# Permuting the q and k columns and adding product blocks before the logits matmuls in the two middle chunks

## The chip, the core and the metric

The kernel runs on one core of a Trainium2 chip. The core has five engines with instruction streams of their own: TensorE (PE in the profile; its weight loads are listed as PEld), VectorE (DVE), ScalarE (ACT), GpSimd (POOL) and SyncE (SP). They meet only at semaphores. Matmul results go to PSUM, all other data lie in SBUF. The metric is the device time of one launch in microseconds. The times before were 264.53, 264.16 and 264.13 us, median 264.16.

## The reference

Input x has 2048 rows (tokens) of 640 elements, type bf16. Two branches work on the layer norm of x, and both are added to x.

```
xn  = layernorm(x)
qkv = xn @ wqkv                       # 32 heads of 20 elements
for token s, head h, w in 0..7:       # window of 8, dilation 2
    logits[s,h,w] = sum_d q[s,h,d] * k[s-2w,h,d] * 20**-0.5   (masked where s-2w < 0)
attn = softmax over w
o[s,h,:] = sum_w attn[s,h,w] * v[s-2w,h,:]
out = x + o @ wo + ((xn @ w_gate) * (xn @ w_up)) @ w_down     # 1536 hidden columns
```

## The kernel before

The 2048 tokens are cut into four chunks of 512, and each chunk into four token tiles of 128. A row of 640 is five blocks of 128 partitions (KT = 5).

For a chunk, TensorE does these things:
- `qk` (L405): q and k, transposed, so that a partition is a column of q or k and the 512 tokens lie along the free dimension. For each of the five blocks, five matmuls of 512 columns. Their weights are 128 neighbouring columns of wq or wk. ScalarE copies the results out of PSUM (L412).
- `vproj` (L438): v, one token tile at a time. It is stored to a scratch tensor vD in HBM, from where VectorE's operand for the values is loaded with the eight window positions side by side (L556, issued on SP).
- the logits (L492, below),
- `glu` (L623): gate and up, 12 pairs of groups of five matmuls. ScalarE copies them out (L628), VectorE multiplies them to hT (L639).
- `down` (L664 and L667): for each token tile, two halves of 320 columns. Each half is 12 matmuls with hT and wd and five with the attention output oT and wo, into one PSUM bank. VectorE adds x on the way out (L674). For the first tile of a chunk the last two hT matmuls of each half come after both halves' other matmuls.

The logits are made in two steps (`prodlog`). VectorE multiplies q by k shifted by 0, 2, ... 14 tokens: eight products of 128 partitions x 2560 elements (five blocks of 512 tokens), two to a tile `pw` (L476). TensorE then sums them over the 20 elements of each head with a selector matrix Ek of zeros and ones: for each block i the selector `Ek[:, i, :]` says which head each of the 128 columns of that block belongs to. A matmul has 32 columns of weights (heads) and 512 of tokens, four of them work side by side in four column strips of the array, and five blocks accumulate. So one group of four products is 20 matmuls, and a chunk has two groups.

ScalarE copies the logits out (L505), the SP queue transposes them (LT, L513), VectorE takes the maximum and subtracts it (L524 to L528), ScalarE takes the exponential, VectorE sums and normalizes (L541 to L546). `av` then multiplies the loaded values by the weights (L581), adds the eight positions in a tree (L590, L594, L596) and a transpose on SP makes oT (L603).

The order of the work is made by a planner. Each step is given with an engine, an estimated cost, its dependencies and sometimes an order. `Plan.order` lists the steps, at each time taking the ready one with the least slack to the end. The logits steps are marked `urgent`: they go first on TensorE as soon as the plan counts them ready, with 0.9 us added after the last product (`margin`). The engines then run their streams in exactly that order. In the order before, the logits of chunk 0 lie before its last v tiles, those of chunk 1 among the q matmuls of chunk 2, those of chunk 2 before the last tile of the chunk-1 down-projection, those of chunk 3 after the first part of the chunk-2 down-projection.

Five buffers (`pv`) hold the four `pw` tiles and one loaded value tile. Value tiles two to four of a chunk go into buffers that the logits matmuls release. Matmul results rotate through six PSUM banks, which ScalarE and VectorE empty.

Of the kernel before, what the change touches and what calls it, by code (L numbers as in the profile page):

```python
# [10 lines left out]
ALU = mybir.AluOpType  # L11
# [20 lines left out]
class Plan:  # L32
# [8 lines left out]
    def add(self, eng, cost, fn, deps=(), occ=None, after=(), kb=0):  # L41
        s = Step(eng, cost, fn, deps, occ, after)
        s.kb = kb
        s.idx = len(self.steps)
        self.steps.append(s)
        return s
# [51 lines left out]
def kernel(  # L98
# [11 lines left out]
    nc = tc.nc  # L110
    P = nc.NUM_PARTITIONS
# [4 lines left out]
    H = 32  # L116
    Dh = D // H
# [5 lines left out]
    KT = D // P  # L123
# [4 lines left out]
    CS = CH * P  # L128
    JL = P // H
    NS = D // 2  # L130
    BF, F32 = dt.bfloat16, dt.float32
    assert D == KT * P and F == FT * P and S == NCH * CS and W * H == 2 * P and Dh == JL * KT

    const = ctx.enter_context(tc.tile_pool(name="const", bufs=1))
# [5 lines left out]
    wq = const.tile([P, KT, D], BF, name="wq")  # L140
    wk = const.tile([P, KT, D], BF, name="wk")
# [4 lines left out]
    wd = const.tile([P, FT, D], BF, name="wd")  # L146
    ident = const.tile([P, P], BF, name="ident")
    mhalf = const.tile([P, 1], F32, name="mhalf")
    Ek = const.tile([P, KT, H], BF, name="Ek")
    negm = const.tile([P, 2, HALO], F32, name="negm")  # L150
    vD = dram.tile([HALO + S, D], BF, name="vD")

# [1 line left out]
    add = plan.add  # L154
    T = {}

    def new(key, shape, dtype, tag, bufs, pool=None):
        t = (pool or sb).tile(shape, dtype, name=tag, tag=tag, bufs=bufs)
        T[key] = t
        return t  # L160
# [10 lines left out]
    def wload(dst, src, eng=None):  # L171
        return lambda: (eng or nc.sync).dma_start(out=dst[:], in_=src.rearrange("(i p) f -> p i f", p=P))
# [31 lines left out]

    def consts_e():
        nc.gpsimd.memset(Ek[:], 1.0)
        nc.gpsimd.affine_select(out=Ek[:], in_=Ek[:], pattern=[[P, KT], [-Dh, H]], compare_op=ALU.is_ge,
                                fill=0.0, base=0, channel_multiplier=1)
        nc.gpsimd.affine_select(out=Ek[:], in_=Ek[:], pattern=[[-P, KT], [Dh, H]], compare_op=ALU.is_ge,
                                fill=0.0, base=Dh - 1, channel_multiplier=-1)  # L210

    def consts_m():
        nc.gpsimd.memset(negm[:], 0.0)
# [95 lines left out]
    def pe_main(cost, fn, deps=(), banks=1):  # L309
        nonlocal main  # L310
        waits = []
        for k in range(banks):
            if len(ring) + k >= 6:
                waits.append(ring[len(ring) + k - 6])
        main = add("PE", cost + 0.165, fn, [main, *waits, *deps], occ=cost)
        return main
# [79 lines left out]
    def qk(c, lo, n, rs=(0, 1)):  # L396
        for r in rs:
            for j in range(KT):
                key = ("qk", c, r, j, lo)

                def pe(i0, i1, key=key, r=r, j=j):
                    if i0 == 0:
                        new(key, [P, 512], F32, "ps", 6, psum)
                    for i in range(i0, i1):
                        nc.tensor.matmul(T[key][:, 0:n], lhsT=(wk if r else wq)[:, i, j * P : (j + 1) * P],  # L405
                                         rhs=T["xnT", c][:, i, lo : lo + n], start=(i == 0), stop=(i == KT - 1))

                def ev(key=key, r=r, j=j):
                    if r == 0 and j == 0 and lo == 0:
                        new(("q", c), [P, KT, CS], BF, "q", 2)  # L410
                    dst = T["k", c][:, j, HALO + lo : HALO + lo + n] if r else T["q", c][:, j, lo : lo + n]
                    nc.scalar.copy(dst, T[key][:, 0:n])  # L412

                one = n / 2400 + 0.0027
                ts = range(c * CH + lo // P, c * CH + (lo + n) // P)
                mine = [WK if r else WQ, *[TX.get(t, TT[t]) for t in ts], LASTPW.get(c - 2)]
                if c or r or j:
                    a = pe_main(KT * one, lambda pe=pe: pe(0, KT), mine + [TT[t] for t in ts])
                else:
                    pe_main(3 * one, lambda pe=pe: pe(0, 3), mine)  # L420
                    a = pe_main(2 * one, lambda pe=pe: pe(3, KT), [TT[t] for t in ts], banks=0)
                e = add("ACT", 0.16 + n / 1200, ev, [a, HALOCP[c]], occ=0.07 + n / 1200)
                ring.append(e)
                (Kk if r else Q).setdefault(c, []).append(e)
# [38 lines left out]


    SPLAST = [None]
    PW, LL, LE, SS, DD, AA, O16, OE, V8, DT = {}, {}, {}, {}, {}, {}, {}, {}, {}, {}

    def prodlog(c):
        for g in range(2):
            for j in range(4):  # L470
                i = 4 * g + j

                def mul(i=i):
                    if i % 2 == 0:
                        new(("pw", c, i // 2), [P, 2, KT, CS], BF, "pv", 5)
                    nc.vector.tensor_tensor(T["pw", c, i // 2][:, i % 2, :, :], T["q", c][:],  # L476
                                            T["k", c][:, :, DIL * i : DIL * i + CS], ALU.mult)

                m = 8 * c + i
                w = [LL.get(2 * c - 1), O16.get(4 * c - 4), O16.get(4 * c - 3), O16.get(4 * c - 2)][i // 2]  # L480
                PW[m] = add("DVE", 1.48, mul, [*Q[c], *Kk[c], w], occ=1.395, after=[PW.get(m - 1) if i else V8.get(4 * c - 1)])
        LASTPW[c] = PW[m]
        if c == 0:
            load_v8(0)
        for g in range(2):
            n = 2 * c + g

            def lg(g=g):
                l = new(("lps", c, g), [P, 512], F32, "pl", 2, psum)
                for i in range(KT):  # L490
                    for j in range(4):
                        nc.tensor.matmul(l[H * j : H * (j + 1), :], lhsT=Ek[:, i, :], rhs=T["pw", c, 2 * g + j // 2][:, j % 2, i, :],  # L492
                                         start=(i == 0), stop=(i == KT - 1), tile_position=(0, H * j),
                                         skip_group_check=True)

            LL[n] = add("PE", 1.25, lg, [PW[m], LL.get(n - 1), LE.get(n - 2), LE.get(n - 1 - g), CE], occ=1.12)
            LL[n].urgent = True
            LL[n].margin = 0.9

            def ev(g=g):  # L500
                L = new(("L", c, g), [P, CS], BF, "L", 2)
                if c == 0:
                    ps = T["lps", c, g]
                    nc.vector.tensor_tensor(ps[:, 0:HALO], ps[:, 0:HALO], negm[:, g, :], ALU.add)
                nc.scalar.copy(L[:], T["lps", c, g][:])  # L505

            LE[n] = add("ACT", 0.585, ev, [LL[n], SS.get(n - 2), CM], occ=0.5)

            def tr(g=g):
                if g == 0:  # L510
                    new(("LT", c), [P, CH, W, H], BF, "LT", 1)
                out = T["LT", c][:].rearrange("p t (g w) h -> p t g (w h)", g=2)[:, :, g, :]
                nc.sync.dma_start_transpose(out=out, in_=T["L", c, g][:])  # L513

            early = [SPLAST[0]] if c == 0 else []
            SS[n] = SPLAST[0] = add("SP", 3.5, tr, [LE[n], DD.get(2 * c - 1), DD.get(2 * c - 2)], occ=1.25, after=early, kb=160)

# [32 lines left out]
    def load_v8(t):  # L550
        def fn():
            v = new(("v8", t), [P, W, D], BF, "pv", 5)
            r0 = t * P
            src = vD[r0 : r0 + P, :]
            src = bass.AP(tensor=src.tensor, offset=src.offset, ap=[[D, P], [DIL * D, W], [1, D]])
            nc.sync.dma_start(out=v[:], in_=src)  # L556
        order = [SPLAST[0]] if t < CH - 1 else [SS[2 * (t // CH) + 1]] if t % CH in (1, 2) else []
        c, u = divmod(t, CH)
        order.append(V8[t - 1] if u else PW[8 * c + 6])
        if t == 3:  # L560
            order.append(WL["o"])
        w = LL[2 * c + (u - 1) // 2] if u else O16.get(t - 1)
        V8[t] = add("SP", 6.0, fn, [VS[t], VS.get(t - 1), w, CZ], occ=0.5, after=order, kb=1280)
        if t < 3:
            SPLAST[0] = V8[t]
            V8[t].floor = (40.0, 0, 0)[t]

    def load_down():
        WL["d"] = SPLAST[0] = add("SP", 8, wload(wd, B_w_down), after=[SPLAST[0]], occ=0.5, kb=1920)

    def load_out():
        WL["o"] = SPLAST[0] = add("SP", 8, wo_load, after=[SPLAST[0]], occ=2.7, kb=1100)

# [134 lines left out]
    a = st_in(0, 0)  # L708
    a = st_in(0, 1, a)
    aggr_in(0, a)  # L710
    a = st_in(1, 0)
    a = st_in(1, 1, a)
# [10 lines left out]
    a = st_in(2, 0)  # L723
    a = st_in(2, 1, a)
# [6 lines left out]
    a = st_in(3, 0)  # L731
    a = st_in(3, 1, a)
# [9 lines left out]
    CE = add("POOL", 1.2, consts_e, [C0, RS[3]])  # L742
# [77 lines left out]
```

## Time and profile before

| | before |
|---|---|
| median of three runs | 264.16 us |
| span of the profiled execution | 263.0 us |
| TensorE busy, of the span | 258.2 us, 98% |
| VectorE busy | 214.6 us, 82% |
| ScalarE busy | 106.1 us, 40% |
| one chunk's logits on TensorE | 2.27 us for 40 matmuls |
| one product on VectorE (L476) | 1484 ns, 32 of them |
| TensorE's granted clock | 1.000 |

The profile gives one execution. Its span runs from the first to the last instruction; it states no device time of its own beside that, and the median of the runs is 1.16 us above the span. "Busy" counts the time in which an engine has an instruction in work; a share of busy time is an average over stages with different limits. The chain that ended last is followed back from the last instruction, at each step to what released it. In groups, the first number behind the bar is the total busy time in us, the second the mean of one in ns, and behind the next bar stands the time that the engine sat idle just before, with the releaser.

### The profile page before, as it was taken

What the parts mean: (1) busy time and instruction counts of PE and PEld (TensorE: products, weight loads), DVE (VectorE), ACT (ScalarE), POOL (GpSimd) and SP (SyncE); (2) the same over time, 40 slices, a digit from 0 to 9 for tenths busy, and PEclk for the clock granted to TensorE, in tenths of its full rate; (3) what the DMA queues carried; (4) which work ended last, traced back from release to release, by engine and by line L of the source; (5) the groups of instructions that cost most, each with busy time, mean ns of one, the idle gap of its engine ahead of it and who ended that gap; (6) DMA issues with size and microseconds to landing.
All of it is one profiled execution on the core that took longest, in us unless ns stands there. A gap on an engine that the chain in (4) does not pass through costs nothing.

```text
span 263.0 us, 4102 instructions
## 1 busy us (share of the span) xinstructions
PE 258.2 (98%) x1574; PEld 140.4 (53%) x1574; DVE 214.6 (82%) x337; ACT 106.1 (40%) x197; POOL 39.4 (15%) x84
## 2 busy tenths in 40 slices
PE   7999999999999999999999999999999999999995
PEld 2645445444577546444477554644456764445763
DVE  5586997999999969999999189999992999993221
ACT  3655557655300258455500155655541105554000
POOL 4551036000031021400001000420000004000000
PEclk9999999999999999999999999999999999999999
DMA  7978997999978139931167299451903995111001
GB/s 217 326 175 231 402 373 171 370 362 244 195 155 270 54 68 370 316 114 27 25 125 250 66 311 319 97 150 25 224 3 75 365 293 134 26 25 25 27 25 50
DMA packets 50707, 46.55 MB, mean 177 GB/s; under 512 B 24786, under 2 KB 47840, under 8 KB 50688
## 3 DMA queue, kind: packets, MB, share of 16 engines
q1 hardware_dynamic: 46704, 37.10, 50.0%
q0 software_dynamic: 2384, 8.05, 9.2%
q10 hardware_dynamic: 1600, 1.15, 1.4%
q8 instruction: 12, 0.20, 0.3%
q14 instruction: 7, 0.06, 0.1%
HBM read 35.39 MB, written 5.26 MB: 155 GB/s over the span
## 4 chain that ended last, share of the span: by engine, by line
PE 94%; DMA 3%; DVE 1%; issue 0%
PE ps L623 39%; PE ps L664 20%; PE ps L405 17%; PE ps L667 8%; PE ps L438 7%; PE pl L492 3%; DMA wq<-in_A_wqkv_dram 3%; DMA x<-in_A_x_dram 1%; DVE st L251 1%; DVE xr L674 0%; DVE mv L257 0%; DVE ve L259 0%; DVE x L270 0%
## 5 line engine op out<-in xcount | busy, mean ns | idle before, releaser
L623 PE MATMUL ps<-xnT,wg 128*128 128x512 bf16 x240 | 59.6, 379 | 0.0
L623 PE MATMUL ps<-xnT,wu 128*128 128x512 bf16 x240 | 59.6, 379 | 0.0
L664 PE MATMUL ps<-wd,hT 128*128 128x320 bf16 (+2 forms) x384 | 57.4, 299 | 0.0
L476 DVE TENSOR_TENSOR pv<-q,k 128x2560 bf16<-128x2560 bf16 x32 | 46.5, 1484 | 1.7 <-ACT k L412 1.7
L664 PEld LDWEIGHTS <-hT 128*128 128x128 bf16 x384 | 37.0, 98 | 16.5 <-issue 0.8
L581 DVE TENSOR_TENSOR pv<-pv,a 128x5120 bf16<-128x5120 bf16 x16 | 45.1, 2819 | 0.1
L628 ACT CAST gs<-ps 128x512 bf16<-128x512 f32 x48 | 28.2, 587 | 32.1 <-PE ps L623 32.1
L623 PEld LDWEIGHTS <-wu 128*128 128x128 bf16 x240 | 23.5, 98 | 28.3
L623 PEld LDWEIGHTS <-wg 128*128 128x128 bf16 x240 | 23.5, 98 | 27.7
L628 ACT CAST us<-ps 128x512 bf16<-128x512 f32 x48 | 28.2, 588 | 22.4 <-PE ps L623 21.4
L674 DVE TENSOR_TENSOR xr<-ps,xr 128x320 bf16<-128x320 f32 (+2 forms) x32 | 15.0, 486 | 24.4 <-PE ps L667 16.1
L667 PE MATMUL ps<-wo,oT 128*128 128x320 bf16 (+2 forms) x160 | 27.0, 299 | 0.0
L698 POOL DMA_DIRECT2D out_dram<-xr x14 | 7.6, 545 | 124.6 <-DVE xr L674 118.0
L590 DVE TENSOR_TENSOR pv<-pv 128x2560 bf16<-128x2560 bf16 x16 | 23.8, 1485 | 0.1
L438 PE MATMUL ps<-wv,xnT 128*128 128x320 bf16 x160 | 23.2, 299 | 0.4 <-ACT xnT L351 0.4
L412 ACT CAST q<-ps 128x512 bf16<-128x512 f32 x20 | 11.7, 586 | 28.3 <-PE ps L405 28.3
L639 DVE TENSOR_TENSOR hT<-gs,us 128x512 bf16<-128x512 bf16 x48 | 19.5, 419 | 4.1 <-ACT us L628 4.1
L405 PE MATMUL ps<-xnT,wq 128*128 128x512 bf16 x100 | 22.4, 379 | 0.4 <-DMA wq<-in_A_wqkv_dram 0.4
L405 PE MATMUL ps<-xnT,wk 128*128 128x512 bf16 x100 | 22.2, 379 | 0.0
L438 PEld LDWEIGHTS <-xnT 128*128 128x128 bf16 x160 | 15.3, 98 | 7.4 <-ACT xnT L351 0.5
L667 PEld LDWEIGHTS <-oT 128*128 128x128 bf16 x160 | 15.5, 98 | 6.3
L251 DVE BATCH_NORM_STATS2 st<-x 128x6 f32<-128x320 bf16 x32 | 13.9, 481 | 4.4 <-DMA x<-in_A_x_dram 4.4
(54 smaller groups left out, 177.4 us busy)
## 6 DMA issues: line engine op xcount, KB each, us to landing
pv<-vD SPq DMA_DIRECT2D x16, 1280.0 KB, 9.9
vD<-v_t POOLq DMA_DIRECT2D x16, 160.0 KB, 4.5
xr<-in_A_x_dram POOLq DMA_DIRECT2D x16, 160.0 KB, 3.6
out_dram<-xr POOLq DMA_DIRECT2D x14, 160.0 KB, 3.7
wg<-in_B_w_gate_dram SPq DMA_DIRECT2D x1, 1920.0 KB, 8.1
wu<-in_B_w_up_dram SPq DMA_DIRECT2D x1, 1920.0 KB, 11.9
wd<-in_B_w_down_dram SPq DMA_DIRECT2D x1, 1920.0 KB, 14.6
x<-in_A_x_dram SPq DMA_DIRECT2D x11, 160.0 KB, 6.8
```

What stands on the lines that cost most here:

```text
L251: nc.vector.bn_stats(T["st", t][:, g, :], T["x", t][:, g * NS : (g + 1) * NS])
L405: nc.tensor.matmul(T[key][:, 0:n], lhsT=(wk if r else wq)[:, i, j * P : (j + 1) * P], rhs=T["xnT", c][:, i, lo : lo + n], start=(i == 0), ...
L438: nc.tensor.matmul(T["psv", t, n][:, 0:NS], lhsT=T["xnT", c][:, i, q * P : (q + 1) * P], rhs=wv[:, i, n * NS : (n + 1) * NS], start=(i == ...
L476: nc.vector.tensor_tensor(T["pw", c, i // 2][:, i % 2, :, :], T["q", c][:], T["k", c][:, :, DIL * i : DIL * i + CS], ALU.mult)
L581: nc.vector.tensor_tensor(v[:].rearrange("p w (j h) -> p w j h", j=Dh, h=H), v[:].rearrange("p w (j h) -> p w j h", j=Dh, h=H), T["a", n][ ...
L590: nc.vector.tensor_tensor(v[:, 0:4, :], v[:, 0:4, :], v[:, 4:8, :], ALU.add)
L623: nc.tensor.matmul(ps[:], lhsT=(wu if r else wg)[:, i, f * P : (f + 1) * P], rhs=T["xnT", c][:, i, :], start=(i == 0), stop=(i == KT - 1))
L628: nc.scalar.copy(s[:], T[key][:])
L639: nc.vector.tensor_tensor(h[:], T["gs", c, f][:], T["us", c, f][:], ALU.mult)
L664: nc.tensor.matmul(ps, lhsT=T["hT", c, f][:, q * P : (q + 1) * P], rhs=wd[:, f, sl], start=(f == 0), stop=(f == FT - 1 and not wo_part))
L667: nc.tensor.matmul(ps, lhsT=T["oT", t][:, g, :], rhs=wo[:, g, sl], start=False, stop=(g == KT - 1 and f1 == FT))
L674: nc.vector.tensor_tensor(T["xr", t][:, sl], T["psD", t, n][:, 0:w], T["xr", t][:, sl], ALU.add)
```

## The change

The weights of q and k are no longer 128 neighbouring columns but every fifth column: block j takes columns j, j + 5, j + 10, and so on. Partition p of block j then holds column 5p + j, which belongs to head p // 4 whatever j is. So one selector of 32 columns serves all five blocks, and blocks may be added to each other, partition by partition, before the selector is applied.

In chunks 1 and 2 (`LEVELS`), after each pair of products, `fold` lets VectorE add blocks 2 and 3 of a `pw` tile to its blocks 0 and 1, in place: one instruction over both products of the tile, 2 x 1024 elements per partition, four instructions in a chunk. The logits of these chunks then sum three blocks (0, 1 and 4) in place of five: 24 matmuls a chunk in place of 40. Chunks 0 and 3 keep five. The path over GpSimd in `fold` and the deeper levels are not used.

The logits step now depends on the folds, and the planner is given its new cost, so the order changes around it. Chunk 1's logits come after 25 q and 15 k matmuls of chunk 2 (before: after 20 q). Chunk 2's come after the whole chunk-1 down-projection and the 25 q matmuls of chunk 3 (before: ahead of the last down tile). Chunk 3's come ahead of the last half tile of the chunk-2 down-projection (before: after the first of its eight halves, of 10 + 5 matmuls). On VectorE the folds of chunk 1 stand together behind its products, those of chunk 2 stand in pairs between evictions, and the first product of the next chunk moves ahead of the softmax sums in chunks 1 and 2. On SP the four xnT transposes of chunk 3 come ahead of the last oT transpose of chunk 1. GpSimd's order is the same.

```diff
-    Ek = const.tile([P, KT, H], BF, name="Ek")
+    Ek = const.tile([P, H], BF, name="Ek")
...
-        nc.gpsimd.affine_select(out=Ek[:], in_=Ek[:], pattern=[[P, KT], [-Dh, H]], compare_op=ALU.is_ge,
+        nc.gpsimd.affine_select(out=Ek[:], in_=Ek[:], pattern=[[-JL, H]], compare_op=ALU.is_ge,
...
-                        nc.tensor.matmul(T[key][:, 0:n], lhsT=(wk if r else wq)[:, i, j * P : (j + 1) * P],
+                        nc.tensor.matmul(T[key][:, 0:n], lhsT=(wk if r else wq)[:, i, :].rearrange("p (c b) -> p c b", b=KT)[:, :, j],
...
+    LEVELS = (0, 1, 1, 0)
+    FOLDER = ('DVE', 'DVE', 'DVE', 'DVE')
+    LEFT = (tuple(range(KT)), (0, 1, KT - 1), (0, KT - 1), (0,))
+    HALVES = ((0, 2, 2, 4), (0, 1, 1, 2), (0, 1, KT - 1, KT))
+
+    def fold(c, u):
+        s = PW[8 * c + 2 * u + 1]
+        for lo, hi, a, b in HALVES[: LEVELS[c]]:
+            def fn(lo=lo, hi=hi, a=a, b=b):
+                w = T["pw", c, u]
+                if FOLDER[c] == "DVE":
+                    nc.vector.tensor_tensor(w[:, :, lo:hi, :], w[:, :, lo:hi, :], w[:, :, a:b, :], ALU.add)
...
+            n = (hi - lo) * 2 * CS
+            if FOLDER[c] == "DVE":
+                s = add("DVE", 0.25 + n / 1920, fn, [s], occ=0.165 + n / 1920)
...
+                if i % 2:
+                    FO[4 * c + i // 2] = fold(c, i // 2)
...
-                for i in range(KT):
+                left = LEFT[LEVELS[c]]
+                for i in left:
                     for j in range(4):
-                        nc.tensor.matmul(l[H * j : H * (j + 1), :], lhsT=Ek[:, i, :], rhs=T["pw", c, 2 * g + j // 2][:, j % 2, i, :],
-                                         start=(i == 0), stop=(i == KT - 1), tile_position=(0, H * j),
+                        nc.tensor.matmul(l[H * j : H * (j + 1), :], lhsT=Ek[:], rhs=T["pw", c, 2 * g + j // 2][:, j % 2, i, :],
+                                         start=(i == left[0]), stop=(i == left[-1]), tile_position=(0, H * j),
...
-            LL[n] = add("PE", 1.25, lg, [PW[m], LL.get(n - 1), LE.get(n - 2), LE.get(n - 1 - g), CE], occ=1.12)
+            took = 0.022 + 0.2195 * len(LEFT[LEVELS[c]])
+            LL[n] = add("PE", took + 0.13, lg, [*[FO[4 * c + u] for u in range(4)], LL.get(n - 1), LE.get(n - 2), LE.get(n - 1 - g), CE], occ=took)
```

More of the change, by code (lines that the diff above doesn't have):

```diff
@@ L206, in consts_e @@
         nc.gpsimd.memset(Ek[:], 1.0)
-        nc.gpsimd.affine_select(out=Ek[:], in_=Ek[:], pattern=[[P, KT], [-Dh, H]], compare_op=ALU.is_ge,
+        nc.gpsimd.affine_select(out=Ek[:], in_=Ek[:], pattern=[[-JL, H]], compare_op=ALU.is_ge,
                                 fill=0.0, base=0, channel_multiplier=1)
-        nc.gpsimd.affine_select(out=Ek[:], in_=Ek[:], pattern=[[-P, KT], [Dh, H]], compare_op=ALU.is_ge,
-                                fill=0.0, base=Dh - 1, channel_multiplier=-1)
+        nc.gpsimd.affine_select(out=Ek[:], in_=Ek[:], pattern=[[JL, H]], compare_op=ALU.is_ge,
+                                fill=0.0, base=JL - 1, channel_multiplier=-1)
     def consts_m():
@@ L465 @@
     SPLAST = [None]
+    FO = {}
     PW, LL, LE, SS, DD, AA, O16, OE, V8, DT = {}, {}, {}, {}, {}, {}, {}, {}, {}, {}
+    LEVELS = (0, 1, 1, 0)
[9 more added lines that the diff above has]
+                    nc.vector.tensor_tensor(w[:, :, lo:hi, :], w[:, :, lo:hi, :], w[:, :, a:b, :], ALU.add)
+                else:
+                    nc.gpsimd.dma_start(out=w[:, :, lo:hi, :], in_=w[:, :, a:b, :], accum_op=ALU.add)
+            n = (hi - lo) * 2 * CS
+            if FOLDER[c] == "DVE":
+                s = add("DVE", 0.25 + n / 1920, fn, [s], occ=0.165 + n / 1920)
+            else:
+                s = add("POOL", 4.0, fn, [s], occ=1.2, kb=n / 4)
+        return s
     def prodlog(c):
```

## The prediction

> **What bounds the kernel now.** First the head of the page, the busy shares, the slices and the chain that ended last.
>
> ```profile
> span 263.0 us, 4102 instructions
> PE 258.2 (98%) x1574; PEld 140.4 (53%) x1574; DVE 214.6 (82%) x337; ACT 106.1 (40%) x197; POOL 39.4 (15%) x84
> ...
> PE   7999999999999999999999999999999999999995
> ...
> DVE  5586997999999969999999189999992999993221
> PEclk9999999999999999999999999999999999999999
> ...
> PE 94%; DMA 3%; DVE 1%; issue 0%
> ```
>
> TensorE holds 94% of the chain, at full granted clock in every slice. VectorE is at nine tenths for long stretches, with holes near slices 23 and 31. So time taken from TensorE is worth its full length, as long as VectorE, which receives new work, still delivers each operand before TensorE asks for it. That is a question of slack at a few places, so I read the chain in order of time next, then VectorE's timeline at the same places (start, duration, then the work; in brackets the idle time before it).
>
> ```profile
> 69.06 1.36 PE ps L664 x10
> ...
> 78.29 1.63 PE ps L664 x12
> ...
> 87.53 4.32 PE ps L405 x20
> 91.85 2.27 PE pl L492 x40
> 94.12 6.58 PE ps L405 x30
> 100.70 5.43 PE ps L438 x40
> 106.13 25.90 PE ps L623 x120
> ...
> 133.39 0.68 PE ps L667 x5
> ...
> 145.89 2.27 PE pl L492 x40
> 148.16 1.74 PE ps L664 x12
> ...
> 169.11 25.90 PE ps L623 x120
> ...
> 197.05 2.27 PE pl L492 x40
> 199.32 1.47 PE ps L664 x10
> ...
> 258.20 1.08 PE ps L667 x5
> ```
>
> ```profile
> 89.18 1.48 DVE L476 TENSOR_TENSOR pv<-q,k 128x2560 bf16<-128x2560 bf16 x1
> 90.58 2.45 DVE L251 BATCH_NORM_STATS2 st<-x 128x6 f32<-128x320 bf16 x6
> ...
> 94.08 1.49 DVE L270 TENSOR_SCALAR x<-x,mv,rstd 128x640 bf16<-128x640 bf16 x3
> 97.54 0.29 DVE L524 TENSOR_TENSOR m<-LT 128x256 bf16<-128x256 bf16 x1 [1.98 <-DMA LT<-L]
> ...
> 103.16 2.83 DVE L581 TENSOR_TENSOR pv<-pv,a 128x5120 bf16<-128x5120 bf16 x1
> ...
> 130.20 0.49 DVE L596 TENSOR_TENSOR o<-pv 128x640 bf16<-128x640 bf16 x1
> ...
> 140.49 0.48 DVE L674 TENSOR_TENSOR xr<-ps,xr 128x320 bf16<-128x320 f32 x1
> 140.89 1.48 DVE L476 TENSOR_TENSOR pv<-q,k 128x2560 bf16<-128x2560 bf16 x1
> ...
> 151.66 0.29 DVE L524 TENSOR_TENSOR m<-LT 128x256 bf16<-128x256 bf16 x1 [0.56 <-DMA LT<-L]
> ```
>
> **The terms.** The groups by shape (busy total, mean ns) carry the prices:
>
> ```profile
> L590 DVE TENSOR_TENSOR pv<-pv 128x2560 bf16<-128x2560 bf16 x16 | 23.8, 1485 | 0.1
> L594 DVE TENSOR_TENSOR pv<-pv 128x1280 bf16<-128x1280 bf16 x16 | 13.1, 821 | 0.2
> L639 DVE TENSOR_TENSOR hT<-gs,us 128x512 bf16<-128x512 bf16 x48 | 19.5, 419 | 4.1 <-ACT us L628 4.1
> L528 DVE TENSOR_TENSOR d<-LT,m 128x512 f32<-128x512 bf16 x8 | 5.5, 692 | 0.3
> L405 PEld LDWEIGHTS <-wk 128*128 128x128 bf16 x100 | 9.8, 98 | 11.8
> L444 ACT CAST v_t<-ps 128x320 bf16<-128x320 f32 x32 | 13.3, 430 | 7.4 <-PE ps L438 4.1 <-DMA vD<-v_t 3.3
> L412 ACT CAST k<-ps 128x512 bf16<-128x512 f32 x20 | 11.7, 586 | 9.4 <-PE ps L405 9.4
> ```
>
> Last, the DMA issues (median us to landing) and two stretches of SP's timeline:
>
> ```profile
> pv<-vD SPq DMA_DIRECT2D x16, 1280.0 KB, 9.9
> ...
> oT<-o SPq DMA_TRANSPOSE x16, 2.8
> ```
>
> ```profile
> 96.40 3.81 SPq L556 DMA_DIRECT2D pv<-vD  x3
> ...
> 132.06 5.16 SPq L339 DMA_TRANSPOSE xnT<-x  x4
> ```
>
> *Removed from TensorE.* A chunk's logits are 40 matmuls in 2.27 us. Chunks 1 and 2 keep 24, so 24/40 x 2.27 = 1.36 us, 0.91 us less each and 1.82 us together. Chunks 0 and 3 keep 40. The 0.1 us lost on returning from logits to other matmuls (1.74 for 12 matmuls at 148.16, 0.11 over the 1.63 of other such groups) stays.
>
> *Added to VectorE.* Four in-place adds of 2048 elements per partition in each of the two chunks. Between the in-place rows of 2560 and 1280 elements the slope is (1485 - 821)/1280 = 0.519 ns, so one takes 1485 - 512 x 0.519 = 1219 ns. Independent neighbours overlap by 0.08 us (the product of 89.18 lasts 1.48 and its successor starts 1.40 later), so one add occupies 1.14 us: 4.56 us per chunk, 9.1 us in all. Bounds: at the f32 row's 512 elements in 692 ns (below one element per ns) an add would be near 692 + 1536/512 x 692 = 2.77 us; at the in-place rate 1.22. I take 1.22, since type, engine and in-place form are those of the nearer rows.
>
> *Weights with a column step of five.* 200 loads of q, k weights now read every fifth column. No row shows a stepped weight load. Packed ones take 98 ns, beside matmuls that start 4.32/20 = 0.216 us apart, so a load is free up to 216 ns. ScalarE's copy of 320 elements with a large step costs 430 ns against 586 for 512 packed ones; the difference, 156 ns for 192 elements or 0.81 ns each, leaves 430 - 320 x 0.81 = 170 fixed, the same as 586 - 512 x 0.81 = 171: there the step is free. By that 98 ns, by a doubling (two elements read for one) 196; both hide, so zero, with nothing on the gain side as packed loads are hidden already. [...] The sum is the same unless the slowed load passes the 216 ns, which is a rival below. No run so far shows it.
>
> *Constants.* The selector shrinks from 160 to 32 columns on POOL, far from the path: zero. Each selector load still precedes its matmul.
>
> **What the new order moves.** The planner puts logits 1 behind 25 q and 15 k matmuls, logits 2 behind the whole chunk-1 down-projection and 25 q matmuls, logits 3 before the last half tile of the chunk-2 down. One product of the following chunk goes ahead of the softmax sums in chunks 1 and 2. I follow VectorE against TensorE, place by place.
>
> *Logits 1.* TensorE reaches them at 87.53 + 40 x 0.216 = 96.17. The products end as before, four adds follow: 90.58 + 3 x 1.14 + 1.22 = 95.22. Slack 0.95, the smallest.
>
> *Softmax and values of chunk 1.* Logits end 97.53. Before, the maximum started 3.42 after their end (94.12 to 97.54: eviction, transpose), so 100.95; VectorE, with its layer norm 4.56 later, is free at 95.57 + 4.56 = 100.1. From maximum to first value multiply 5.62, plus the inserted product 1.40, less the idle 0.23 it fills: 107.7. From there to the last output 27.53 (103.16 to 130.69), plus two more hT multiplies (0.42 less the overlap each), 0.67: 135.9. TensorE finishes gate and up at 106.13 - 0.91 + 25.90 = 131.12. It needs the tenth hT then; What follows that hT on VectorE is 0.82 + 0.49 + 2.83 + 0.67 + 1.49 + 0.82 + 0.49, with overlaps 7.5, so it is ready at 128.4, slack 2.7. The value loads of token tiles two to four, which need the logits' buffers, are issued 2.3 us after the logits' end as before (96.40), so from 99.8; the second multiply comes at 107.7 + 5.7 = 113.4, 13.6 later, against 9.9 to landing. The last output's transpose, now queued on SP behind four xnT transposes that wait for gate and up to finish (131.1 plus 5.16 us of issue, the row at 132.06), leaves at 136.4 and lands 2.8 later, before about 146.6 when the last token tile asks for it.
>
> *Logits 2.* Down lasted 87.53 - 69.06 = 18.47, so it ends at 149.59; 25 q matmuls more, 154.99. VectorE from 135.9: 7 products x 1.40, 8 evictions x 0.40, 4 adds x 1.14 = 17.6, hence 153.5, or 153.6 with the last add's tail. Slack 1.4. TensorE then runs 1.36 + 0.1 + 5.39 + 5.43 to gate and up at 167.3 (169.11 before), ending 193.2.
>
> *Values of chunk 2.* Maximum at 156.35 + 3.50 = 159.85, values from 166.6, last output 194.8. Behind the tenth hT stand 1.49 + 0.82 + 0.49 and two hT, 3.4 with overlaps: 191.4 against 193.2, slack 1.8.
>
> *Chunk 3.* Its products end near 206.4; logits 3 start at 193.18 + 18.47 - 2.31 (a half tile, 1.63 + 0.68) = 209.34, slack 2.9. Their end 211.61 is 12.3 later than before. Maximum at 215.0, last output at 215.0 + 5.39 + 27.53 + 0.67 = 248.6, its transpose 2.8 later, 251.4. TensorE needs it for the group that stood at 258.20, now 256.4: slack 5. So what falls late everywhere is VectorE, and TensorE meets each operand in time.
>
> **The sum.** The span is 263.0 - 1.82 = 261.2. The profiled execution shows no device time of its own beside the span; the runs shown have a median of 264.16, 1.16 above it, which I keep: 262.34. About 0.2% of the time, 0.53 us, is what can be told from no change.
>
> **The rivals.**
>
> *VectorE comes late (faster by little, or no change).* For: slacks of 0.95 and 1.4 where nine tenths are busy, and logits 3 moved by 12 us. Against: the adds are of a shape well bracketed, and all other waits keep 1.8 or more. Adds priced like the 2560 row (1.49) would take 4 x 1.40 = 5.6 and end at 96.3, a stall of 0.1. A further lateness of 1 us at two places costs up to 1.5: 262.8 to 264.5.
>
> *A weight load longer than its matmul (slower).* The place is the 200 q, k loads, each beside a 216 ns matmul. A load of L costs 200 x (L - 216) ns on TensorE; from 225 ns on it eats the 1.82. At three times the packed time, 294 ns, it costs 15.6 us: 262.34 + 15.6 = 277.9; at 235 ns 266.1. For: nothing in the trace shows a stepped load. Against: more than a doubling is needed. [...]
>
> *Adds at f32 rate (slower or level).* 2.77 us each puts logits 1 at 90.58 + 11.0 = 101.6, a stall of 5.4, and part of it again at logits 2: 264.16 - 1.82 + 5.4 = 267.7 or more. Against: both in-place bf16 rows.
>
> *The change does less than it says.* If four matmuls side by side cost more per group when fewer follow, the gain is under 0.91 a chunk; even at half of it 263.25.
>
> **How the numbers follow.** The forecast, 262.34, has 0.71, its own range 262.0 to 262.8. VectorE late 0.13, spread evenly from 262.8 to 264.5. The smaller gain 0.03. Weight loads 0.08 and slow adds 0.05, above 264.7. The range 261.9 to 264.4 leaves out the two slower cases and a little. Faster takes the forecast, the smaller gain and about half of the late case, 0.80; no change the rest of the late case, 0.07; slower 0.13.
>
> **What would show it.** Adds near 1.22 us, x8. Logits groups of 24 in 1.36 us, starting near 96.2 and 155.0, with TensorE's wait list empty of VectorE there. Weight loads on the q, k line near 98 and below 216 ns, their 50 matmuls still 10.8 us per chunk. Maximum of chunk 3 near 215, last output near 249, the last tile's first wo group near 256.4. A wait of TensorE for VectorE at logits or at the down-projection, or q, k matmuls spaced beyond 0.216, would make the prediction wrong.

## The result and the profile after

The changed kernel takes 262.63 us in the median of four runs (262.45 to 263.31), beside 264.33 for the kernel before (264.13 to 264.53, four runs). The ratio is 0.994, with a 95% interval of 0.9926 to 0.9955: 1.70 us less. The forecast was 262.3.

The head of the page of the changed kernel, with the lines that answer to those shown of before:

```profile
span 261.6 us, 4046 instructions
PE 256.6 (98%) x1542; PEld 143.7 (55%) x1542; DVE 223.0 (85%) x345; ACT 104.8 (40%) x197; POOL 38.8 (15%) x84
...
DVE  5586996999999995999999973989999819999941
PEclk9999999999999999999999999999999999999999
...
PE 90%; DMA 5%; DVE 4%; POOL 0%; issue 0%; SPq 0%
```

TensorE has 32 matmuls less and still holds the chain. VectorE has 8.4 us more busy time. Its two holes have moved with the later logits, from slice 23 to 25, where it is now three tenths busy and not one, and from slice 31 to 33. The part of the chain outside TensorE grew in the first 25 us: chunk 0's logits start at 36.99 here and at 36.70 before. That is not the work of the new order, for two kernels of the experiments with the same order start them at 36.03 and 36.37. From the start of these logits to the end of the span it is 226.3 us before and 224.6 now, 1.7 us less. This profiled execution, 263.31 us, is also the longest of the four. It lies 1.7 us above its span, as the profiled execution of the first experiment does (264.02 over 262.3). With 1.7 the profiled execution of before, span 263.0, would be one of 264.7 us, longer than the four timed. So the 1.16 us that the prediction kept between span and median probably paired a longer execution with the median of others. Only differences went into the sum, so nothing hung on it.

The chain in order of time, changed kernel (start, duration, work):

```profile
87.81 8.63 PE ps L405 x40
96.45 1.41 PE pl L517 x24
97.86 2.29 PE ps L405 x10
100.14 5.43 PE ps L438 x40
105.58 25.90 PE ps L649 x120
...
155.34 1.41 PE pl L517 x24
...
167.71 25.90 PE ps L649 x120
193.61 1.36 PE ps L690 x10
...
209.77 2.27 PE pl L517 x40
...
256.81 1.08 PE ps L693 x5
```

Logits of 24 matmuls take 1.41 us, not 1.36. Between 2.27 for 40 and 1.41 for 24 a matmul is worth 0.86/16 = 0.054 us, and 0.12 us a chunk does not shrink (16 take 0.98 us in the kernel with two adds in both middle chunks, as the two terms give). So the gain is 2 x 0.86 = 1.72 us. The medians show 1.70, closer than four runs a side can tell: the 23 runs of before that were timed beside the first experiments have a median of 264.13, 1.50 above the changed kernel. TensorE waits for nothing at any of these places.

VectorE's timeline at the places of the prediction, changed kernel:

```profile
91.24 4.62 DVE L480 TENSOR_TENSOR pv<-pv 128x2048 bf16<-128x2048 bf16 x4
...
103.28 0.29 DVE L550 TENSOR_TENSOR m<-LT 128x256 bf16<-128x256 bf16 x1 [2.53 <-DMA LT<-L]
...
137.97 0.88 DVE L700 TENSOR_TENSOR xr<-ps,xr 128x320 bf16<-128x320 f32 x2
...
153.25 2.35 DVE L480 TENSOR_TENSOR pv<-pv 128x2048 bf16<-128x2048 bf16 x2
160.68 0.29 DVE L550 TENSOR_TENSOR m<-LT 128x256 bf16<-128x256 bf16 x1 [5.09 <-DMA LT<-L]
...
192.45 0.42 DVE L665 TENSOR_TENSOR hT<-gs,us 128x512 bf16<-128x512 bf16 x1
...
248.47 0.49 DVE L622 TENSOR_TENSOR o<-pv 128x640 bf16<-128x640 bf16 x1
```

The adds of chunk 1 end at 95.86, 0.59 ahead of the logits. Those of chunk 2 end at 155.60, which is 0.26 after the logits of chunk 2 have started. TensorE did not wait there all the same: the last add belongs to the second group of logits, which starts 0.7 us after the first, so 0.45 us was left. The tenth hT of chunk 2 is ready at 192.87, 0.74 before TensorE's down-projection at 193.61.

And the groups of the two things that had no or no exact row before:

```profile
L405 PEld LDWEIGHTS <-wk 128*128 128x128 bf16 x100 | 11.6, 118 | 10.3 <-issue 0.8
...
L480 DVE TENSOR_TENSOR pv<-pv 128x2048 bf16<-128x2048 bf16 x8 | 9.3, 1214 | 0.0
```

### The profile page after: what moved, and what is told of

It reads as the page before. It is cut to its first block, busy times and chain, and to the rows that moved or that the text cites. A ratio compares the mean times of both kernels' runs of the same rounds, so it can differ in the third digit from the quotient of the medians.

```text
span 261.6 us, 4046 instructions
## 1 busy us (share of the span) xinstructions
PE 256.6 (98%) x1542; PEld 143.7 (55%) x1542; DVE 223.0 (85%) x345; ACT 104.8 (40%) x197; POOL 38.8 (15%) x84
## 4 chain that ended last, share of the span: by engine, by line
PE 90%; DMA 5%; DVE 4%; POOL 0%; issue 0%; SPq 0%
PE ps L649 40%; PE ps L690 20%; PE ps L405 13%; PE ps L693 8%; PE ps L438 6%; DMA x<-in_A_x_dram 4%; PE pl L517 3%; DVE st L251 2%; DMA xnT<-x 1%; DVE x L270 1%; POOL rstd L265 0%; DVE mv L257 0%; DVE ve L259 0%; DVE xr L700 0%; SPq L172 0%
```

## The experiments

The reading to be tested: the gain is TensorE's 32 matmuls and nothing else; adds, permutation and new order are free, the adds only just. The rivals: the permutation or the order gains or costs; the adds are paid in part; VectorE has far more slack than it seems.

### One part alone: the permutation

```diff
-    LEVELS = (0, 1, 1, 0)
+    LEVELS = (0, 0, 0, 0)
```

> The columns of wq and wk permuted and the one selector, no block added, five blocks in all logits, order of work as before. Theory (the gain is the 32 logits matmuls taken from TensorE, a stepped weight load is hidden): the time before, 264.2 to 264.4; the q, k loads 118 ns as in the changed kernel's profile, their matmuls 0.216 us apart, a chunk's 50 in 10.8 us. Rival 'stepped loads cost': above 264.9. Rival 'the permutation itself gains' (fewer selector bytes, other order of loads): near 262.6.

Measured: 264.11 us beside 264.13, ratio 1.0001 (0.999 to 1.0011). TensorE's order is that of before, and its 50 q, k matmuls of a chunk take 10.79 us, as before. The load takes longer and none of it shows:

```profile
L405 PE MATMUL ps<-xnT,wk 128*128 128x512 bf16 x100 | 22.2, 379 | 0.0
...
L405 PEld LDWEIGHTS <-wk 128*128 128x128 bf16 x100 | 11.7, 117 | 9.8
```

The permutation by itself neither gains nor costs.

### One part alone: adds and new order, all five blocks summed

```diff
-                left = LEFT[LEVELS[c]]
+                left = LEFT[0]
```

> The changed kernel with its adds and its order of work, but all five blocks are summed in chunks 1 and 2 as well, so blocks 2 and 3 count twice in the logits there. Theory (32 matmuls are worth 1.72 us of TensorE, adds and order are free): 262.63 + 1.72 = 264.35, logits of 40 in 2.27 us. Rival 'adds or new order cost something that the gain covers': above 264.7. Rival 'the new order is what gains': near 262.6.

Measured: 264.25 us beside 264.13, ratio 1.0005 (0.9996 to 1.0014), logits 2.27 us again. With the 32 matmuls put back the gain is gone, and the adds and the order cost nothing that can be told. The order is not what gains.

### One part taken out: no adds

```diff
-                    nc.vector.tensor_tensor(w[:, :, lo:hi, :], w[:, :, lo:hi, :], w[:, :, a:b, :], ALU.add)
+                    pass
```

> The changed kernel with the eight adds left out: blocks 2 and 3 are missing from the logits of chunks 1 and 2, 24 matmuls there. Theory (adds lie in VectorE's slack): the time of the changed kernel, 262.4 to 262.8. Rival 'adds are paid in part': below 262.3, at most 0.9 us of gain in addition per chunk if VectorE were the bound there.

Measured: 262.69 us beside 264.13, ratio 0.9939 (0.9926 to 0.9951), against 0.994 with the adds. 9.3 us of VectorE work more or less do not move the end. VectorE's idle time at the maximum of chunks 1 and 2 is 7.95 and 9.44 us here, 2.53 and 5.09 with the adds: that is where they fit in. The two rows without the adds:

```profile
102.95 0.29 DVE L550 TENSOR_TENSOR m<-LT 128x256 bf16<-128x256 bf16 x1 [7.95 <-DMA LT<-L]
...
160.16 0.29 DVE L550 TENSOR_TENSOR m<-LT 128x256 bf16<-128x256 bf16 x1 [9.44 <-DMA LT<-L]
```

### The suspected cost doubled: each add twice

```diff
                     nc.vector.tensor_tensor(w[:, :, lo:hi, :], w[:, :, lo:hi, :], w[:, :, a:b, :], ALU.add)
+                    nc.vector.tensor_tensor(w[:, :, lo:hi, :], w[:, :, lo:hi, :], w[:, :, lo:hi, :], ALU.max)
```

> Every add is followed by a second instruction of the same size on the same data (maximum of a block with itself, which changes nothing), order of work unchanged, so VectorE gets 4.56 us more in each middle chunk. Theory (the slack at logits 1 and 2 is what is left, read from the changed kernel's trace as 0.6 and 0.4 us for the second group of logits): logits 1 wait for VectorE about 3.3 us in their second group, logits 2 another 3 to 4; time 262.6 + 6 to 7.4 = 268.6 to 270.0. Rival 'VectorE has far more slack than the page suggests': 262.6 to 263.5.

Measured: 271.19 us (270.94 and 271.43), 8.56 more than the changed kernel, 1.2 more than expected. TensorE's timeline of this run at both logits:

```profile
95.52 0.83 PE L518 MATMUL pl<-pv,Ek 128*32 128x512 bf16 x12
97.11 0.39 PE L518 MATMUL pl<-pv,Ek 128*32 128x512 bf16 x2 [0.76 <-DVE pv L481]
99.50 0.82 PE L518 MATMUL pl<-pv,Ek 128*32 128x512 bf16 x10 [2.00 <-DVE pv L481]
...
157.75 0.83 PE L518 MATMUL pl<-pv,Ek 128*32 128x512 bf16 x12
159.51 0.39 PE L518 MATMUL pl<-pv,Ek 128*32 128x512 bf16 x2 [0.93 <-DVE pv L481]
161.90 0.84 PE L518 MATMUL pl<-pv,Ek 128*32 128x512 bf16 x10 [2.00 <-DVE pv L481]
162.67 7.20 PE L405 MATMUL ps<-xnT,wk 128*128 128x512 bf16 x25
```

The waits are where and about as long as expected, and in two steps, one for each `pw` tile of the second group. Logits 1 last from 95.52 to 100.32 and logits 2 from 157.75 to 162.74: 3.3 and 3.5 us over the 1.48 that the same view gives for either in the changed kernel. The rest is the last line: 25 k matmuls take 7.13 us of the chain where the changed kernel needs 5.52. The same run by stretches (columns: stretch, length and TensorE's busy time, then the other engines, the granted clock, the DMA share and GB/s):

```profile
161.90:162.74 0.84, 0.84 (x11) 0.30 (x11) 0.00 (x0) 0.00 (x0) 0.00 (x0) 0.91 0.00 0
162.74:164.00 1.26, 1.26 (x5) 0.45 (x5) 0.00 (x0) 0.59 (x1) 0.00 (x0) 0.50 0.00 0
164.00:166.00 2.00, 2.00 (x6) 0.70 (x5) 0.05 (x1) 0.59 (x1) 0.00 (x0) 0.50 0.41 72
166.00:168.00 2.00, 2.00 (x11) 1.07 (x10) 1.83 (x6) 0.83 (x2) 0.00 (x0) 1.00 0.83 273
```

The granted clock fell to a half for some 3.3 us after the second pair of waits, and 1.61 us went there. 3.3 + 3.5 + 1.6 = 8.4, nearly the whole of the 8.56 between the medians. Between the two profiled executions it is all: from the start of logits 1 (96.38 in this view of the changed kernel) to the end of the span it is 173.7 us here and 165.2 there, 8.5 more. So the slack was real and as small as read.

### The suspected load, slower: a column step of twelve

```diff
-                        nc.tensor.matmul(ps[:], lhsT=(wu if r else wg)[:, i, f * P : (f + 1) * P],
+                        nc.tensor.matmul(ps[:], lhsT=(wu if r else wg)[:, i, :].rearrange("p (c b) -> p c b", b=FT)[:, :, f],
...
-        WL["d"] = SPLAST[0] = add("SP", 8, wload(wd, B_w_down), after=[SPLAST[0]], occ=0.5, kb=1920)
+        WL["d"] = SPLAST[0] = add("SP", 8, lambda: nc.sync.dma_start(out=wd[:], in_=B_w_down.rearrange("(p i) f -> p i f", p=P)), after=[SPLAST[0]], occ=0.5, kb=1920)
```

> The changed kernel, and the weights of gate and up are read with a column step of twelve too (hidden column 12 c + f in partition c of block f, w_down laid out to match, twelve rows together per partition): 480 loads whose neighbouring elements lie 24 bytes apart, none two in the same 16 bytes. Theory (a stepped load costs some 20 ns as with step five, and is hidden below 216 ns): load 118 to 200 ns, time of the changed kernel, 262.3 to 262.9. Rival 'loads exposed': above 216 ns, 480 x (load - 216); at 250 ns 278.9. [...]

Measured: 262.75 us (262.44 to 263.68) beside 264.12, ratio 0.9946 (0.9932 to 0.996): the time of the changed kernel. Two rows of its groups:

```profile
L649 PEld LDWEIGHTS <-wu 128*128 128x128 bf16 x240 | 23.5, 98 | 28.3
```

is the packed load of the changed kernel, and with the step of twelve:

```profile
L649 PEld LDWEIGHTS <-wu 128*128 128x128 bf16 x240 | 34.3, 143 | 17.5
```

98, 118 and 143 ns for steps of one, five and twelve. All stay below the 216 ns at which the matmuls beside them follow each other (120 in 25.90 us), and 480 loads of the slowest kind left no trace in the median. The rival of the exposed load is settled for these loads beside 512-column matmuls; none came near 216 ns, so what happens there was not seen. The profiled execution, 263.68 us, is the longest of the nine, and TensorE waited in it once:

```profile
110.10 1.24 PE L649 MATMUL ps<-xnT,wg 128*128 128x512 bf16 x5 [0.99 <-ACT v_t L444]
```

This is no weight load. ScalarE's copy of v was late, because a store of v to vD (8.04 us in the chain) still held its buffer. Waits for v_t come up again below.

### More of the same: where it stops

Five kernels take away more logits matmuls. Each needs the number in `LEVELS` alone: two adds in both middle chunks (0, 2, 2, 0), the add in the last three chunks (0, 1, 1, 1), in all four (1, 1, 1, 1), and mixed (0, 1, 2, 0) and (0, 2, 1, 0). The planner orders each anew.

> In chunks 1 and 2 a second add (block 1 to block 0, 2 x 512 elements per partition) after the first, so the logits sum two blocks: 16 matmuls a chunk; the planner orders anew and puts both logits behind all q, k and one v group. Theory (each logits matmul taken away is worth 0.86/16 = 0.054 us while VectorE still comes in time; 48 fewer than before): 264.13 - 48 x 0.054 = 261.5 us. Rival 'VectorE late': adds cost 4 x (1.14 + 0.61) = 7.0 us a chunk and the logits come 2.5 to 5 us later than in the changed kernel, so a wait of TensorE for hT at the down-projection or for the last oT eats it: 262.6 to 266.

> The add also in chunk 3: 24 matmuls in chunks 1, 2 and 3; logits 3 move behind the whole chunk-2 down-projection. Theory: 264.13 - 3 x 0.86 = 261.55, with the last output near 250 to 251 and TensorE still asking for its transpose near 256. Rival 'VectorE late in chunk 3' (4.56 us more work before its softmax): above 262.4, with a wait of TensorE at the last down-projection.

> The add in all four chunks: 24 matmuls everywhere; logits 0 move behind all v tiles of chunk 0 and 1, logits 1 behind half of the v tiles. Theory: 264.13 - 4 x 0.86 = 260.7 us. Rival 'chunk 0 has no slack': VectorE, which holds layer norms and products there, delays hT of chunk 0 and with it the first down-projection; above 262, with waits of TensorE in the first 90 us.

> Chunk 1 as in the changed kernel (24 matmuls), chunk 2 with the second add (16 matmuls), chunks 0 and 3 with 40; the planner puts logits 2 behind 15 k matmuls and logits 3 behind the whole chunk-2 down-projection, and hT multiplies of chunk 2 further ahead. Theory (40 logits matmuls fewer at 0.054 us, VectorE still in time): 264.13 - 2.15 = 262.0. Rival 'the slack is used up' (the changed kernel's tenth hT of chunk 2 was ready only 0.7 us before TensorE asked): a wait at a down-projection of 0.5 to 3 us, 262.5 to 265.

> The second add in chunk 1 in place of chunk 2 (16 and 24 matmuls). Theory: 262.0 if VectorE comes in time in chunk 1. Rival: the run with two levels in both chunks waited 0.3 us for hT in chunk 1 and 1.6 at the last down-projection, where logits 3 came as late as here or later; by that 262.3 to 264.

| `LEVELS` | logits matmuls fewer | worth at 0.054 | expected if hidden | measured | ratio and interval | TensorE's waits in the profiled execution |
|---|---|---|---|---|---|---|
| 0, 1, 1, 0 | 32 | 1.72 | | 262.63 | 0.994 (0.9926 to 0.9955) | none |
| 0, 2, 1, 0 | 40 | 2.15 | 262.0 | 262.87 | 0.9953 (0.9938 to 0.9967) | 0.52 for v_t, 0.16 |
| 0, 2, 2, 0 | 48 | 2.58 | 261.5 | 263.58 | 0.9981 (0.9971 to 0.9991) | 0.29 and 1.58 for hT |
| 0, 1, 1, 1 | 48 | 2.58 | 261.55 | 264.21 | 1.0006 (0.998 to 1.0031) | 2.11 for hT |
| 0, 1, 2, 0 | 40 | 2.15 | 262.0 | 266.33 | 1.0075 (1.0053 to 1.0098) | 1.17 and 1.31 for hT, 0.83 for v_t, 0.16 |
| 1, 1, 1, 1 | 64 | 3.44 | 260.7 | 270.05 | 1.0213 (1.0177 to 1.0248) | 1.58 for oT, 2.26 and 1.16 for hT |

In four of the five TensorE waits at a down-projection, as the rivals said. With the add in all four chunks the wait in the first 90 us is one for oT, at 80.34, and not one for hT. (0, 1, 2, 0) lies above even its rival's 262.5 to 265 and waits for v_t as well. In (0, 2, 1, 0) no wait for hT appears; its 262.87 lies in the rival's 262.3 to 264, with a wait for v_t. The waits as TensorE's timelines show them, with two adds in both middle chunks:

```profile
134.74 2.21 PE L690 MATMUL ps<-wd,hT 128*128 128x320 bf16 x15 [0.29 <-DVE hT L665]
...
244.79 2.55 PE L690 MATMUL ps<-wd,hT 128*128 128x320 bf16 x16 [1.58 <-DVE hT L665]
```

and with (0, 1, 2, 0):

```profile
171.52 1.24 PE L649 MATMUL ps<-xnT,wg 128*128 128x512 bf16 x5 [0.83 <-ACT v_t L444]
198.64 2.21 PE L690 MATMUL ps<-wd,hT 128*128 128x320 bf16 x15 [1.17 <-DVE hT L665]
...
246.89 2.55 PE L690 MATMUL ps<-wd,hT 128*128 128x320 bf16 x16 [1.31 <-DVE hT L665]
```

For the kernel with (0, 2, 2, 0) the sum comes close to the median: 264.12 - 2.58 + 1.87 = 263.4 against 263.58; the profiled execution itself took 264.04. For (0, 1, 1, 1) it gives 264.12 - 2.58 + 2.11 = 263.65, and the profiled execution took 264.53; the runs spread from 263.43 to 266.1. With (0, 2, 1, 0) the 0.43 us more came back as 0.68 us of waits, 0.52 of them for ScalarE's copy of v, which empties TensorE's banks. The execution with the step of twelve shows such a wait too, in the changed kernel's order, so it is not shown that the second add makes it. This kernel is not told apart from the changed one. For (0, 1, 2, 0) and all four chunks the listed waits are 3.5 and 5.0 us of the 4.1 and 8.2 us that the profiled executions (266.17 and 268.86) lie above the sum without waits; in the latter the granted clock was 0.72 from 244 to 250, some 1.7 us more, and the remainder is not accounted for. No version beat the changed kernel.

## Why the prediction was right

The sign, the size and the mechanism held: TensorE's time in the logits is worth its length, and everything put on VectorE fits into its slack. Its steps one by one:

- *Removed from TensorE.* Right in kind, 0.05 us a chunk too large: 0.86, not 0.91, since 0.12 us of a chunk's logits does not scale with the matmuls. So the gain was 1.72 by the chain and 1.70 by the medians, and not 1.82; that is 0.12 of the 0.29 us by which the time came out above 262.34. The rest, 0.17, is the median of before, 264.33 with a fourth run and 264.16 without. The rival 'the change does less than it says' came true in this small part. Putting the matmuls back took the gain away.
- *Added to VectorE.* The adds take 1214 ns (forecast 1219), 4.62 us for four in a row (4.56 plus the last one's tail).
- *Weights with a column step of five.* Hidden, as forecast. The value taken, 98 ns, was too low; 118 was measured, inside the bounds of 98 and 196. That a load is free up to 216 ns was the author's estimate; the slowest stepped loads of the runs took 143 ns in the mean. The working for 98 proved nothing: the 0.81 ns an element was got by supposing the same fixed time in ScalarE's two rows, so that 170 and 171 came out alike says nothing of the step.
- *The new order.* TensorE's places came as worked out, shifted by the 0.28 us of the first stage: logits 1 at 96.45 (96.17), logits 2 at 155.34 (154.99), logits 3 at 209.77 (209.34), the last tile's first wo group at 256.81 (256.4).
- *The slacks.* At logits 1 it was 0.59 and not 0.95: the adds start at 91.24, which is 0.38 later than the shift of 0.28 explains. Behind that one term was mis-sized. The prediction took 3.42 us from the end of logits 1 to the first maximum. It was 5.42 (97.86 to 103.28). VectorE was therefore 2.0 us late from there to the evictions of chunk 1, 137.97 and not 135.9. The tenth hT of chunk 1 had 0.9 us where 2.7 was forecast (ready at 130.59, asked for at 131.48), and the slack of 1.4 at logits 2 was gone. That TensorE met no wait there was luck, as far as the prediction goes: it did not use that a group of logits waits only for its own two tiles. In chunk 2 the same stretch was 3.93, not 3.50, and the tenth hT had 0.74 us where 1.8 was forecast. Chunk 3 came as worked out: last output at 248.96 (248.6).
- *The rival 'VectorE comes late'* was nearer than its 0.13 suggests: the smallest slack left was 0.45 us, and the doubled adds and four of the five kernels above ran into waits for VectorE. *The exposed load* and *adds at f32 rate* did not happen.

Part of the longer stretch can be worked out from SP's timeline, before (L513) and after (L539), chunks 1 and 2:

```profile
93.73 2.50 SPq L513 DMA_TRANSPOSE LT<-L  x2
...
147.77 2.51 SPq L513 DMA_TRANSPOSE LT<-L  x2
```

```profile
97.90 2.50 SPq L539 DMA_TRANSPOSE LT<-L  x2
...
156.79 2.51 SPq L539 DMA_TRANSPOSE LT<-L  x2
```

The first transpose follows the first of a chunk's two groups of logits. With 40 matmuls that group ends 2.27/2 = 1.13 us before the logits do, with 24 only 0.70. So the transpose leaves 0.43 later against the end of the logits: 0.39 ahead of it before (93.73 against 94.12), 0.04 behind it now (97.90 against 97.86). This is the whole of chunk 2's 3.93 over 3.50 and 0.43 of the 2.0 in chunk 1. The other 1.6 lie between the issue of the first transpose and the maximum, and their cause stays open. In chunk 1 this took 3.8 us in the two kernels with the old order, 5.38 in the changed kernel and 4.3 to 5.7 in the eight others with a new order (the doubled adds left aside, where the second group waits). So it goes with the order, but in chunk 2 of the changed kernel it was 3.89 again. The longest transpose of logits took 4.0 us to land there, against 2.8 before. No run took the loads beside it away.

## What to carry to other kernels

Work taken off the engine that holds the chain paid its full length here, 1.70 us measured for 1.72 taken, where the engine that receives work stayed ahead at every place where the first one asks, by 0.45 us at the least. So walk these places in the new order of work and subtract: here the smallest of the differences, 0.45 us, told how little more could be moved (the eight adds doubled cost 8.56 us), and the busy share did not. VectorE was busy 82% of the span and still took 9.3 us for nothing (262.63 us with the adds, 262.69 without), while a second add in both middle chunks (2.4 us a chunk by the estimate) brought 1.87 us of waits at the down-projection. Stepped weight loads of 118 and 143 ns beside matmuls that start 216 ns apart cost nothing: 264.11 us beside 264.13 with the step of five alone, 262.75 beside 262.63 with the step of twelve added.

## What the runs showed that was not expected

- *After one pair of waits the granted clock fell, and that cost more time.* In the run with doubled adds, waits of 0.93 and 2.00 us at logits 2, with two matmuls between them, were followed by 3.3 us at a granted clock of 0.50, 1.6 us lost in addition. Waits of 0.76 and 2.00 us at logits 1 of the same run were followed by none: the 10 k matmuls behind them start 0.22 us apart. What made the difference between the two places is not shown.
- *The time of a stepped weight load grew slowly:* 98, 118, 143 ns for steps of one, five and twelve bf16 elements.
- *From the issue of the transposes of chunk 1's logits to the maximum it took 3.8 us* in the old order and 4.3 to 5.7 in the new ones, with the same instructions; the cause is open.
